# Attention of all units by heads in two row halves of TensorE, with the written order searched anew

## The chip, the cores and the metric
One core of a Trainium2 chip. The time is device microseconds of one execution of the kernel; the median of three runs stands for it. Engines: TensorE (PE; PEld is its weight loads), VectorE (DVE), ScalarE (ACT), GpSimd (POOL), and the queue of the transfers on SyncE (SP).

## What is computed
A gated linear attention (mLSTM) over 2 batches, 8 heads, 768 steps and 40 dimensions, and two MLPs behind it on its 1536 x 320 output:

```python
for t in range(S):
    m_new = maximum(f_gate[t] + m, i_gate[t])
    f_stab, i_stab = exp(f_gate[t] + m - m_new), exp(i_gate[t] - m_new)
    C = f_stab * C + i_stab * outer(v[t], k[t])
    n = f_stab * n + i_stab * k[t]
    y[t] = sigmoid(o_gate[t]) * (C @ q[t]) / max(abs(n @ q[t]), 1)
x = (x @ w_a * (x @ w_b)) @ w_out          # 320 -> 1536 -> 320
x = silu(x @ w_in) @ w_out                 # 320 -> 2048 -> 320
```

## The kernel before
Time is cut into 6 chunks of 128 steps; a chunk of one batch is a unit (u0 to u11, batch = u mod 2). A unit's attention is: a matrix of decays (`fb_u` by matmul for units 0 to 3 and loaded from `fsd` for the others, then a scan on VectorE); scores, that is keys times queries per head (L508, L503); the scores weighed by the decays on VectorE (`weigh`, L514); their product with the values (L443); the part carried from the chunk before, queries times state (`carried`, L529); the update of the state (`update`, L539); and the combination, normalisation and output gate on VectorE, ScalarE and GpSimd. A transpose (`px`, L626) then makes x columns for the MLP, split into a high and a low fp32r part (`x_high`, `x_low` L638).

Heads lie in three groups (`GH` = 0, 3, 5) of 3 heads, 120 rows. Scores of one head need the other two heads' rows to be zero. For units 0 to 5 (`u < PLAIN`) the keys are placed by three loads (L221) into two tiles `kz` that were set to zero once (L766), and the product is fp32 with 120 rows and 128 columns. For units 6 to 11 keys and queries are loaded stacked (L215, four transfers each), cast to fp32r (`stack_high`), the rest of 40 rows subtracted on GpSimd (`stack_low`), and one fp32r product of 120 rows gives the scores. The carried part multiplies 120 rows of queries by the state of three heads at once, 123 or 82 columns wide; the update makes 120 x 123 for a group, of which a mask (`bmask`) keeps the three diagonal blocks (L548). The values are multiplied in two column halves of 64 (`halves`):

```python
for c in (slice(0, P // 2), slice(P // 2, m)):
    nc.tensor.matmul(out=out_[c], lhsT=x[:, c], rhs=y, start=True, stop=True)
```

An fp32 matmul leaves two records on TensorE in the profile, an fp32r matmul or a transpose one. All PSUM tiles (`bank`) share eight banks.

The first MLP runs in passes over blocks of 2, 2, 2, 3, 3 units and ranges of its 12 hidden slices (`m0` to `m10`), the second over three blocks of 4 units and 16 slices (`n0` to `n2`). A slice has first products (L657), a gate, a high and a low part on ScalarE and GpSimd, and second products (L666 to L668) that add into `acc`. Weights are loaded as fp64 words and narrowed on ScalarE and VectorE, and split into high and low parts on ScalarE and GpSimd (`split_w1`, `split_w2`, L282).

The order of all instructions is written out in `ORDER`: each word is a step (`u3.s0` scores, `u3.w0` weigh, `u3.v0` values, `u3.car` carried part, `u3.upd` update, `l3.k` a load, `w4.o1` a step of a weight's split, `m0.2.b` a product, `f7` four filler matmuls, L437). Each engine and the SP queue takes its own instructions in that order.

Of the kernel before, what the change touches and what calls it, by code (L numbers as in the profile page):

```python
# [8 lines left out]
F32 = mybir.dt.float32  # L9
# [32 lines left out]
m0.1.b m0.0.e m0.1.a l3.t u3.d1 u3.d0 u3.sv u3.sk w3.p w3.s1 w3.o1 w3.s0 w3.o0 l5.k u3.s0 u3.w0 u2.sig u2.om u3.s1  # L42
u3.w1 u2.da u2.dn w2.v0 u2.rc u2.ox w3.h:p w3.la w3.u m0.2.a m0.2.e m0.2.g w3.t m0.2.h u3.sig u3.upd u3.am u3.cb
u3.v1 u3.v0 u3.cc u3.da m0.0.b m0.0.g m0.0.h lw6 l5.e l5.q w4.v0 m0.2.l u5.s1 u5.s0 m0.2.c lw5 w5.p u2.xt u2.px
u3.dn u3.om u3.rc u3.ox u3.xt u3.px m0.0.l m0.0.c m0.1.e m0.4.a u5.d0 l5.t u5.sk w3.lb u3.ae u2.xh u3.xh u3.xl u2.xl
m1.0.a m1.0.e m0.1.g m0.1.h u5.sv m0.1.l u5.w0 m1.0.b m1.0.g u5.w1 l4.k w3.v0 m0.3.a w5.s1 w5.o1 w6.s1 u5.sig m0.3.e
w3.v1 m0.3.b m0.3.g m0.4.e u5.car u5.cb m1.1.a m1.1.e:v l4.e w4.v1 m0.4.b l4.t u4.sv u5.ao l4.q u4.car u4.s1 m0.3.h
m0.3.l u4.s0 m0.3.c u4.d0 u4.sk w5.s0 w5.o0 w5.h:p w5.la w5.u m0.1.c u5.si u5.v1 w6.p u4.w0 m1.0.h w5.lb m1.0.l
w6.o1 u4.w1 w6.s0 u4.si u4.v0 u4.v1 w6.o0 u4.cb u4.cc u4.sig u4.om w6.t:p u4.upd u5.upd w6.h w6.lb u4.am m0.4.g
m0.4.h:p m0.4.l u4.da u4.dn u4.rc u5.v0 u5.cc u5.da u5.om w6.la u5.am m1.1.b m1.1.g m1.2.a w5.t u4.ox m1.3.a  # L50
m1.3.e:v l6.sk u6.hk u6.lk u5.dn u5.rc m1.2.b m1.2.e m1.2.g u5.ox m0.4.c m1.4.b m1.4.a m1.3.b lw7 w7.s0 w7.p w7.o0
w7.s1 w7.o1 u5.xt l6.t l7.e w5.v0 l6.q w7.h u4.xt:p m1.1.h:p m1.1.l u4.px u4.xh:v u5.px m0.z1 m1.0.c m1.1.c u5.xh
u5.xl u4.xl m2.3.b m2.1.a w6.u w7.la m1.4.e m1.4.g m2.3.a m1.2.h m1.2.l m0.z0 m1.2.c u5.ae m2.1.b m1.4.h:p w7.lb
m1.4.l m1.4.c lw8 w8.s1 u6.sig m2.3.e:v m2.3.g u6.sv m2.4.a m1.3.g m2.1.e:v m2.3.h m2.3.l m2.3.c m2.1.g w8.p w8.s0
w8.o0 l6.e w5.v1 u6.d0 w7.u m1.3.h m1.3.l m2.1.h m2.1.l m1.3.c m1.z0 m2.4.b m2.4.e m2.4.g m2.4.h:p w7.t w8.o1 m2.0.b
lw9 w9.s1 w9.p m2.0.a m2.0.e w9.o1 w6.v0 m3.6.a w9.s0 w9.o0 m3.5.a m2.4.l m2.4.c m2.2.b u4.ao u4.ae w7.v1 m4.7.b
m2.0.g m2.0.h:p m2.0.l u7.d0 m2.2.a w9.h m2.2.e m2.2.g l7.t w6.v1 l6.sq u6.hq u7.sig m2.1.c m2.0.c w7.v0 m3.7.a
m3.7.e w8.h w9.t m3.6.e:v m3.6.b m3.6.g m3.5.e:v m2.2.h:p m2.2.l m2.2.c m2.z0 m2.z1 m3.6.h u6.lq w9.lb m3.6.l w9.la
u7.si:p u6.sk m3.5.b m3.5.g u6.si m3.5.h m4.5.a u6.s0 m4.7.a m4.7.e:v m4.7.g m3.5.l w8.la m3.6.c m3.7.b m4.5.b w9.u
# [24 lines left out]
u11.rc m9.9.l m9.9.c m9.6.l m9.6.c u10.xt:p u11.om u11.ox u11.xt:p u10.px u10.xh:v u10.xl u11.px close lx3 m9.4.a
m9.3.b m9.4.e m9.4.g m9.4.h:p u11.xh y4.xt m9.8.a m9.4.l m9.3.a m9.3.e u11.xl m10.2.a m9.3.g m9.3.h m9.3.l y1.px
y1.xh y1.xl x3.p x3.s x3.o x3.ho x3.lo m9.11.a m9.11.e:v m9.3.c x3.h x3.t x3.l m9.7.b m9.7.g m9.7.h m9.7.l y0.px
y0.xh m10.2.e:v m9.11.b y0.xl m9.11.g lx0 x0.p x0.s x0.o m9.8.b y2.px y2.xh m9.4.c x0.h x0.ho m9.7.c m10.0.b
m9.11.h:p m9.11.l m9.11.c m9.8.e:v m9.8.g m9.8.h m9.8.l m9.8.c lx1 x1.p x1.s x1.o x1.h x1.l x1.t x1.ho x1.lo m9.z0
m9.z1 m9.z2 m10.0.a m10.0.e:v m10.0.g m10.0.h m10.0.l x0.t lx2 x2.p x2.s x2.o x0.l m10.1.b m10.6.a x2.h x2.t x2.l
x0.lo m10.8.b y3.px m10.8.a m10.1.a m10.8.e m10.8.g x2.ho x2.lo m10.8.h m10.8.l m10.0.c y2.xl y3.xh y3.xl n0.0.b  # L90
n0.0.g m10.1.e:v m10.1.g m10.1.h:p m10.1.l lx10 x10.p x10.s lx5 x5.p x10.o n0.0.h x10.ho x10.h x10.l m10.4.b m10.2.b
# [36 lines left out]
def tile_mlstm_gated_mlps(ctx: ExitStack, tc: tile.TileContext, i_gate, f_gate, q_cols, k_cols, kvo, w1, w2,  # L128
# [8 lines left out]
    NT = B * NC  # L137
    DV = D + 1
    G = 3
    GR = G * D  # L140
    GH = (0, 3, 5)
    SLOT = {h: (h // G, h % G) if h < 6 else (2, h - 5) for h in range(H)}
    BLOCKS = {1: (2, 2, 2, 3, 3), 2: (4, 4, 4)}
# [303 lines left out]
    def chunk(u):  # L447
# [74 lines left out]
        def carried():  # L522
            if c == 0:
                return
# [360 lines left out]
```

## Time and profile before

| | |
|---|---|
| median of three runs | 454.04 us (453.29 to 454.51) |
| profiled execution, its own time | 453.9 us |
| its span | 452.2 us |
| PE busy | 445.7 us (99%) |
| PEld busy | 425.2 us (94%) |
| DVE, ACT, POOL busy | 175.3, 192.7, 275.6 us |
| transfers | 46.81 MB |

The span is that of the instructions of one profiled execution; its own time has 1.7 us around it. In the chain of waits each piece of time is given to the instruction that the end waited for, followed back from the last one; the time of a TensorE piece there runs from end to end of matmuls, so a change between tile shapes is in the piece behind it.

### The profile page before, as it was taken

Reading aid. Unit: us, or ns where it says so; the run is one execution under the profiler, and the core shown is the slowest. Engines: PE = TensorE matmul, PEld = TensorE weight load, DVE = VectorE, ACT = ScalarE, POOL = GpSimd, SP = SyncE. Lnnn points to the kernel's source line nnn. Section 1 sums busy time; section 2 is a strip of 40 time slices with the busy share of each in tenths; the row PEclk is TensorE's granted clock in tenths of the full one; section 3 lists DMA queues with packets and bytes.
Section 4 is the critical chain, followed back from the end, with each engine's and each line's share of the span. In section 5 each row is a group of like instructions: output and inputs, shape, how many; then the busy total and the mean of one; then the engine's idle time right before and its main releaser. Section 6 shows DMA issues by size and latency. Waiting matters only on the chain.

```text
span 452.2 us, 8280 instructions
## 1 busy us (share of the span) xinstructions
PE 445.7 (99%) x3279; PEld 425.2 (94%) x3279; DVE 175.3 (39%) x306; ACT 192.7 (43%) x386; POOL 275.6 (61%) x314
## 2 busy tenths in 40 slices
PE   7999999999999999999999999999999999999996
PEld 7999999999999999999999999989899998999896
DVE  7878785733574554654544144231200000000000
ACT  4565555643531334213545444454543323253233
POOL 4589679687887998582575756646633243343342
PEclk9989999999999999999999999999999999999999
DMA  8689549622563284800333233221010000010001
GB/s 261 208 265 304 170 140 291 182 64 88 170 163 101 85 216 107 238 1 1 129 128 129 65 129 97 97 73 56 0 56 4 1 1 1 0 59 0 1 0 59
DMA packets 25422, 46.81 MB, mean 104 GB/s; under 512 B 2344, under 2 KB 20088, under 8 KB 25384
## 3 DMA queue, kind: packets, MB, share of 16 engines
q1 hardware_dynamic: 25384, 46.29, 33.2%
q8 instruction: 26, 0.43, 0.4%
q14 instruction: 12, 0.10, 0.1%
HBM read 43.47 MB, written 2.02 MB: 101 GB/s over the span
## 4 chain that ended last, share of the span: by engine, by line
PE 98%; POOL 0%; ACT 0%; DVE 0%; issue 0%; ACTq 0%; POOLq 0%
PE h L657 50%; PE acc L666 11%; PE acc L668 11%; PE acc L667 11%; PE y_u L443 3%; PE s_u L508 3%; PE warm L437 2%; PE fb_u L461 2%; PE px_u L626 2%; PE ups_u L539 2%; PE y_u L529 1%; PE s_u L503 1%; POOL g2w L282 0%; PE pgb L428 0%; PE pg L419 0%
## 5 line engine op out<-in xcount | busy, mean ns | idle before, releaser
L657 PE MATMUL h<-xring,w_j 128*128 128x256 f32 (+2 forms) x1088 | 179.0, 316 | 0.0
L657 PEld LDWEIGHTS h<-xring,w_j 128*128 128x128 f32 x1088 | 161.5, 190 | 5.0
L282 POOL TENSOR_TENSOR g2w<-gw,g2w 128x512 fp32r<-128x512 f32 x48 | 61.9, 1293 | 82.2 <-ACT g2w L277 74.2
L282 POOL TENSOR_TENSOR w_j<-cvt_j,w_j 128x320 fp32r<-128x320 f32 (+3 forms) x72 | 60.2, 842 | 25.8 <-ACT w_j L277 23.8
L282 POOL TENSOR_TENSOR g<-g,g 128x256 fp32r<-128x256 f32 (+1 forms) x60 | 53.6, 897 | 19.9 <-ACT g L277 18.2
L657 PE MATMUL h<-xeven,w_j 128*128 128x512 f32 x256 | 62.9, 392 | 0.0
L668 PE MATMUL acc<-w_j,g2w 128*128 128x320 f32 x192 | 59.5, 310 | 0.1
L666 PE MATMUL acc<-w_j,g2w 128*128 128x320 f32 x192 | 59.4, 310 | 0.0
L667 PE MATMUL acc<-w_j,g2w 128*128 128x320 f32 x192 | 59.3, 309 | 0.0
L657 PEld LDWEIGHTS h<-xeven,w_j 128*128 128x128 f32 x256 | 47.0, 188 | 8.7
L702 ACT ACTIVATE gw<-h 128x512 f32<-128x512 f32 x48 | 28.1, 596 | 49.1 <-PE h L657 46.7
L700 DVE TENSOR_TENSOR g<-a,h 128x256 f32<-128x256 f32 (+1 forms) x60 | 28.1, 472 | 49.7 <-PE h L657 28.9
L277 ACT CAST g2w<-gw 128x512 fp32r<-128x512 f32 x48 | 29.7, 620 | 39.1 <-PE acc L668 38.8
L666 PE MATMUL acc<-w_j,g 128*128 128x320 f32 x144 | 45.7, 317 | 0.0
L277 ACT CAST g<-g 128x256 fp32r<-128x256 f32 (+1 forms) x43 | 19.0, 443 | 61.2 <-DVE g L700 37.9
L668 PE MATMUL acc<-w_j,g 128*128 128x320 f32 x144 | 44.5, 309 | 0.0
L667 PE MATMUL acc<-w_j,g 128*128 128x320 f32 x144 | 44.4, 308 | 0.0
L666 PEld LDWEIGHTS acc<-w_j,g2w 128*128 128x128 f32 x192 | 36.1, 188 | 1.1
L667 PEld LDWEIGHTS acc<-w_j,g2w 128*128 128x128 f32 x192 | 36.0, 188 | 1.1
L668 PEld LDWEIGHTS acc<-w_j,g2w 128*128 128x128 f32 x192 | 36.0, 188 | 0.4 <-POOL g2w L282 0.4
L282 POOL TENSOR_TENSOR sh_u<-st_u,sh_u 40x1152 fp32r<-40x1152 f32 x12 | 33.6, 2803 | 3.2 <-issue 2.2
L277 ACT CAST w_j<-cvt_j 128x320 fp32r<-128x320 f32 (+3 forms) x48 | 24.7, 537 | 20.9 <-DVE cvt_j L268 15.1
(104 smaller groups left out, 572.7 us busy)
## 6 DMA issues: line engine op xcount, KB each, us to landing
raw_j<-in_w_dram SPq DMA_DIRECT2D x16, 704.0 KB
raw_j<-in_w_dram SPq DMA_DIRECT2D x11, 960.0 KB
kvo_u<-in_kvo_dram SPq DMA_DIRECT2D x12, 480.0 KB
e_u<-fsd SPq DMA_DIRECT2D x8, 512.0 KB
qT_u<-in_q_cols_dram SPq DMA_DIRECT2D x12, 180.0 KB
st_u<-in_k_cols_dram SPq DMA_DIRECT2D x12, 180.0 KB
st_u<-in_q_cols_dram SPq DMA_DIRECT2D x12, 180.0 KB
out_dram<-osb SPq DMA_DIRECT2D x12, 160.0 KB
```

The costliest lines, as they stand in the source:

```text
L277: nc.scalar.copy(out=out_, in_=in_)
L282: (nc.vector if how.get("e") == "v" else nc.gpsimd).tensor_tensor(out=out_, in0=x, in1=y, op=op)
L437: nc.tensor.matmul(out=un["warm"], lhsT=idb, rhs=idb, start=True, stop=True)
L443: nc.tensor.matmul(out=out_[c], lhsT=x[:, c], rhs=y, start=True, stop=True)
L461: nc.tensor.matmul(out=f[:, i], lhsT=ident[:, r:r + 1].to_broadcast([P, P]), rhs=scratch[1][:, s_], start=True, stop=True)
L508: nc.tensor.matmul(out=s[:, i], lhsT=kz[u % 2][:, j, g], rhs=un["q", u][:, g], start=True, stop=True)
L657: nc.tensor.matmul(out=po, lhsT=w[:, wi:wi + P], rhs=xt[:, :, xi], start=(n == 0), stop=(n == len(pairs) - 1))
L666: nc.tensor.matmul(out=o, lhsT=hi, rhs=w[:, off[0]:off[0] + DM], start=first, stop=False)
L667: nc.tensor.matmul(out=o, lhsT=hi, rhs=w[:, off[1]:off[1] + DM], start=False, stop=False)
L668: nc.tensor.matmul(out=o, lhsT=lo, rhs=w[:, off[0]:off[0] + DM], start=False, stop=last)
L700: nc.vector.tensor_tensor(out=Q[j], in0=A.pop(j), in1=PB.pop(j), op=ALU.mult)
L702: nc.scalar.activation(out=Q[j], in_=PB.pop(j), func=ACT.Silu, scale=1 / WS)
```

## The change
Keys and queries of all units are loaded by heads into one tile: heads 0 to 3 in rows 0 to 39, heads 4 to 7 in rows 64 to 103. Scores are fp32 for all units and go in pairs, a head of the lower rows and one of the upper, into two banks. The carried part is one product for a head and a half of the time steps: four tiles of 64 x 64. The state is kept per head (104 rows, 4 heads); the update goes per head into column halves, and needs no mask. The result y has a bank for each half of the heads, with the values' part and the carried part beside each other, and is combined in halves. The memsets, masks, stacks, casts and subtractions go.

The order is another one throughout; the products of the MLPs, the fillers (30 steps) and the loads of weights are the same in number. The attention steps of TensorE that use less than the whole array stand in these stretches (between two of them stand products of the whole array; pg is the columns of the gates):

```text
before: pg0 | u0.v1 | u0.v0 | pg1 | u1.v0 u1.v1 | u2.v1 | u2.v0 | u3.v1 u3.v0 | u5.v1 u4.v0 u4.v1 | u5.v0 |
 u6.v0 | u6.v1 | u7.v1 | u7.v0 | u8.v0 u8.v1 | u9.v1 | u9.v0 | u10.v0 u10.v1 | u11.v0 | u11.v1
after: pg0 | u0.s0 | u0.upd u0.v1 u0.v0 | u1.s0 | pg1 | u1.upd u1.v1 u1.v0 u2.car | u2.s0 | u2.v0 u2.upd u2.v1 |
 u3.car u3.s0 | u3.upd u3.v0 u3.v1 | u5.s0 | u4.s0 u5.car u4.car | u5.v1 u5.v0 u4.upd u4.v1 u4.v0 u5.upd |
 u6.s0 u6.car | u6.v0 u6.v1 u6.upd | u7.car u7.s0 | u7.v0 u7.v1 u8.s0 | u8.car u8.upd u8.v0 u8.v1 u7.upd |
 u9.car u9.s0 u10.s0 u9.v0 u9.upd u9.v1 | u10.car | u10.v0 u10.v1 u11.car u11.s0 | u11.v1 u11.v0
```

The beginning of the order (of the order before two pieces, as far as the first product of the first MLP) and the core of the rest:

```diff
 ORDER = """
-lf const zeros f11 f20 f2 f5 f29 f18 f0 f4 f10 f6 f15 f8 f12 f17 li run0 run1 expf0 expi0 u0.f0 pg0 f13 u0.d0 f28 f7
-u1.si:p f19 u0.f1 u0.d1 f23 f24 u1.f0 f1 f3 lw0.a w0.pa w0.s0 w0.o0 expi1 sel lw0.b l0.q l0.t u0.sv expf1 w0.pb
-w0.s1 w0.o1 l0.k u0.si u0.s1 f9 f16 l1.t f22 u0.s0 u0.sig u0.sk u0.w1 u0.w0 f26 f14 f21 u0.v1 lw1 w1.p w1.s0 w1.s1
...
-w2.h w2.u u2.si u0.xl u2.f1 u2.d1 u1.upd u1.am u2.sk u1.v0 u1.v1 u1.cb u1.da u1.dn u1.om u1.rc u2.s1 w2.lb u2.w1
-u1.ox u1.xt:p w2.la u2.s0 u2.w0 u2.upd u2.am u2.ae lw4 u3.si w4.s0 w4.s1 w4.p w4.o1 w4.o0 w4.t:p w1.v0 u2.v1 u1.px
-u1.xh u1.xl l3.q u3.car l3.k u2.car u2.v0 u3.ao lw3 m0.0.a w2.v1 m0.2.b w1.v1 w4.h w4.la w4.lb w4.u u2.cb u2.cc
...
+lf const f18 f19 f14 f23 f3 f29 f0 f5 f2 sel li run0 f26 f17 run1 expi0 pg0 f16 expf0 f20 u0.f0 u0.d0 f25 f1 u0.f1
+u0.d1 u1.f0 f10 l1.t u1.sv lw0.a w0.pa w0.s0 w0.o0 l0.t u0.si:p u0.sv lw0.b w0.s1 l0.k u0.s0 f11 lw1 u0.sk u0.upd
+expi1 w0.pb w0.o1 u0.w1 u0.v1 l1.k l2.k expf1 u0.sig u0.w0 u0.v0 u0.cb0 f22 f24 starts u1.d0 prod u1.f1 u1.si:p
+u1.s0 f27 w1.p w1.s1 w1.o1 u0.cb1 u0.om u0.da u0.dn u0.am u0.rc u0.ox f9 w0.h w0.u w0.lb w0.la w1.s0 w1.o0 w1.h
+w1.lb u2.f1 f8 u2.d1 u1.d1 u2.f0 f21 u2.d0 u1.sk u1.w1 w1.u w1.la u1.w0 pg1 u2.ao f28 f13 u4.si:p u0.xt w0.t u1.sig
+lw2 w2.p u1.upd u1.am w2.s0 w1.t w2.s1 w2.o1 w2.t:p w2.o0 u1.v1 u1.cb1 u1.v0 u1.cb0 u1.om u1.da u1.dn l2.t u2.sk
+w0.v1 w0.v0 u2.car u2.cb0 u1.rc u2.cb1 u1.ox f4 u2.s0 u2.w1 u2.w0 f12 f6 u3.f0 f15 u3.d0 f7 lw4 w4.p w4.s1 w4.o1
+w4.s0 w4.o0 u2.si u1.xt u1.px u1.xh u1.xl u2.sv u2.v0 u2.upd u2.v1 u0.px u0.xh u2.sig u0.xl u3.f1 u3.d1 u2.cc0
+w2.h:p w2.u w2.lb w2.la w1.v1 lw3 w3.p w3.s1 w3.o1 u2.cc1 w1.v0 w4.h:p w4.u w4.la u3.si:p m0.0.b m0.0.a m0.0.e
...
-    PLAIN = 6
+    HP = P // 2
+    HR = HP + D
+    HG = H // 2
...
+    SLOT = (0, 2, 4, 1, 0, 2, 1, 3)
+    ROWS = (slice(0, D), slice(HP, HR))

     def load_k(u):
         b, c, s = place(u)
-        for j in range(G):
-            r = slice(j * D, (j + 1) * D)
-            nc.sync.dma_start(out=kz[u % 2][r, j], in_=k_cols[b, c, r])
+        t = at.tile([P, 2, 2 * G, C], F32, tag="qk", name=f"qk_u{u}")
+        un["qk", u] = [t[r] for r in ROWS]
+        for x, cols in ((1, k_cols), (0, q_cols)):
+            src = cols[b, c].rearrange("(j d) g t -> d j (g t)", j=G)
+            lower, upper = (h[:, x].rearrange("p (j g) t -> p j (g t)", g=2) for h in un["qk", u])
+            nc.sync.dma_start(out=lower, in_=src[:, :, 0:2 * C])
+            nc.sync.dma_start(out=upper[:, 0:2], in_=src[:, 1:G, C:G * C])
...
         for b in range(B):
-            for g in range(G):
-                nc.tensor.matmul(out=p[:, b * G + g], lhsT=sel[:, b, g].rearrange("p j d -> p (j d)"),
-                                 rhs=last, start=True, stop=True)
+            for n in range(HG):
+                nc.tensor.matmul(out=p[:, b * HG + n], lhsT=sel[:, b, n], rhs=last, start=True, stop=True)
         nc.vector.tensor_copy(out=gb, in_=p)
...
+        def scores():
+            T["s"] = [bank(f"s_u{u}", P, HG, C) for _ in range(2)]
+            for n in range(HG):
+                for half, x in enumerate(un["qk", u]):
+                    i = SLOT[half * HG + n]
+                    nc.tensor.matmul(out=T["s"][half][:, n], lhsT=x[:, 1, i], rhs=x[:, 0, i], start=True, stop=True)
...
+        def y_banks():
+            if "Y" not in T:
+                T["Y"] = [bank(f"y_u{u}", P, 2, HG, DV) for _ in range(2)]
+            return T["Y"]
+
+        COLS = (slice(0, HP), slice(HP, P))

         def values(n):
-            if "y1" not in T:
-                T["y1"] = bank(f"y1_u{u}", P, H, DV)
-            for h in range(4 * n, 4 * n + 4):
-                halves(T["y1"][:, h], un["e", u][:, h], T["v"][:, h])
+            y1 = y_banks()[n]
+            for i in range(HG):
+                for t in COLS:
+                    nc.tensor.matmul(out=y1[t, 0, i], lhsT=un["e", u][:, n * HG + i, t], rhs=T["v"][:, n * HG + i],
+                                     start=True, stop=True)

         def carried():
-            if c == 0:
-                return
-            y2 = bank(f"y2_u{u}", P, H, DV)
-            cb = state[u - B]
-            for g in range(G):
-                lo = 1 if g == 2 else 0
-                nc.tensor.matmul(out=y2[:, GH[g] + lo:GH[g] + G], lhsT=un["q", u][:, g],
-                                 rhs=cb[:, g, lo:G], start=True, stop=True)
-            T["y2"] = y2
+            Y = y_banks()
+            for n in range(HG):
+                for half, x in enumerate(un["qk", u]):
+                    for t in COLS:
+                        nc.tensor.matmul(out=Y[half][t, 1, n], lhsT=x[:, 0, SLOT[half * HG + n], t],
+                                         rhs=state[u - B][ROWS[half], n], start=True, stop=True)

         def update():
-            if c == NC - 1:
-                return
-            T["ups"] = ups = bank(f"ups_u{u}", GR, G, G, DV)
+            T["ups"] = ups = bank(f"ups_u{u}", HR, HG, DV)
             kw = un["k", u].rearrange("p h d -> p (h d)")
-            for g in range(G):
-                nc.tensor.matmul(out=ups[:, g], lhsT=kw[:, GH[g] * D:GH[g] * D + GR],
-                                 rhs=T["v"][:, GH[g]:GH[g] + G], start=True, stop=True)
+            for n in range(HG):
+                for lo, hi, h in ((0, HP, n), (HP, HR, HG + n)):
+                    nc.tensor.matmul(out=ups[lo:hi, n], lhsT=kw[:, h * D:h * D + hi - lo], rhs=T["v"][:, h],
+                                     start=True, stop=True)

         def adv_tile():
             if "cn" not in T:
-                T["cn"] = state[u] = at.tile([GR, G, G, DV], F32, tag=f"cn{b}", name=f"cn_u{u}")
+                T["cn"] = state[u] = at.tile([HR, HG, DV], F32, tag=f"cn{b}", name=f"cn_u{u}")
             return T["cn"]

-        def adv_mask():
-            nc.vector.tensor_tensor(out=adv_tile(), in0=T["ups"], in1=bmask[0:GR], op=ALU.mult)
-
-        def old_tile():
-            if "cd" not in T:
-                T["cd"] = at1.tile([GR, G, G, DV], F32, tag="cd", name=f"cd_u{u}")
-            return T["cd"]
+        def adv_first():
+            nc.vector.tensor_copy(out=adv_tile(), in_=T["ups"])

         def adv_old():
-            gbu = gb[:, b * G:(b + 1) * G, c:c + 1].to_broadcast([GR, G, G * DV])
-            both(old_tile().rearrange("p g j d -> p g (j d)"),
-                 state[u - B].rearrange("p g j d -> p g (j d)"), gbu, ALU.mult)
+            T["cd"] = cd = at.tile([HR, HG, DV], F32, tag="cd", name=f"cd_u{u}", bufs=1)
+            both(cd, state[u - B], gb[:, b * HG:(b + 1) * HG, c:c + 1].to_broadcast([HR, HG, DV]), ALU.mult)

         def adv_end():
-            both(T["cn"], T["cn"], T["cd"], ALU.add)
+            nc.vector.tensor_tensor(out=adv_tile(), in0=T["ups"], in1=T["cd"], op=ALU.add)
...
-        def combine():
-            T["y"] = y = at.tile([P, H, DV], F32, tag="y", name=f"y_u{u}")
+        def combine(n):
+            if "y" not in T:
+                T["y"] = at.tile([P, H, DV], F32, tag="y", name=f"y_u{u}", bufs=2)
+            h = slice(n * HG, (n + 1) * HG)
+            y = T["y"][:, h]
             if c == 0:
-                copy(y, T["y1"])
+                copy(y, T["Y"][n][:, 0])
             else:
-                nc.vector.tensor_tensor(out=y, in0=T["y2"],
-                                        in1=gsb.unsqueeze(2).to_broadcast([P, H, DV]), op=ALU.mult)
-
-        def combine_add():
-            nc.vector.tensor_tensor(out=T["y"], in0=T["y"], in1=T["y1"], op=ALU.add)
+                nc.vector.tensor_tensor(out=y, in0=T["Y"][n][:, 1],
+                                        in1=gsb[:, h].unsqueeze(2).to_broadcast([P, HG, DV]), op=ALU.mult)
+
+        def combine_add(n):
+            y = T["y"][:, n * HG:(n + 1) * HG]
+            nc.vector.tensor_tensor(out=y, in0=y, in1=T["Y"][n][:, 0], op=ALU.add)
...
```

In `load_k` the SP queue gets four transfers a unit in place of those of L199, L221 and L215. The scaling of keys and values, the decays, the norm and the gate work as before.

## Rows read from the trace of the kernel before

**Rows 1.** The page's chain, shares of the span by line.

```profile
PE h L657 50%; PE acc L666 11%; PE acc L668 11%; PE acc L667 11%; PE y_u L443 3%; PE s_u L508 3%; PE warm L437 2%; PE fb_u L461 2%; PE px_u L626 2%; PE ups_u L539 2%; PE y_u L529 1%; PE s_u L503 1%; POOL g2w L282 0%; PE pgb L428 0%; PE pg L419 0%
```

**Rows 2.** Waits of PE and PEld: us in total, times, longest.

```profile
PE warm L437 <- DVE idb L745: 2.5, 1, 2.5
...
PEld acc L668 <- POOL g2w L282: 0.4, 1, 0.4
```

**Rows 3.** Stretches: PE, PEld, DVE, ACT, POOL busy, clock, DMA share, GB/s.

```profile
0.00:36.00 36.00, 33.46 (x388) 32.35 (x389) 29.13 (x51) 20.59 (x36) 22.45 (x47) 0.95 0.75 246
36.00:204.00 168.00, 168.00 (x1484) 165.42 (x1485) 98.32 (x185) 68.11 (x149) 136.17 (x147) 1.00 0.53 153
320.00:449.00 129.00, 128.21 (x724) 116.38 (x722) 2.23 (x4) 49.05 (x94) 50.30 (x42) 1.00 0.03 11
0.00:10.00 10.00, 7.46 (x86) 7.31 (x87) 8.00 (x14) 4.16 (x8) 3.97 (x17) 1.00 0.78 240
23.00:26.60 3.60, 3.60 (x20) 3.60 (x19) 2.53 (x4) 1.92 (x3) 3.60 (x5) 0.53 0.90 283
```

**Rows 4.** The chain in order of time: start us, us, what.

```profile
12.37 0.95 PE s_u L508 x8
13.32 0.67 PE warm L437 x12
...
20.46 1.25 PE pgb L428 x12
...
35.89 1.14 PE h L657 x8
...
39.90 1.79 PE s_u L508 x16
41.69 0.96 PE h L657 x8
42.65 0.63 PE ups_u L539 x6
43.28 1.06 PE y_u L443 x32
44.34 1.15 PE h L657 x8
...
54.49 0.63 PE y_u L529 x6
...
102.62 0.60 PE y_u L443 x16
...
104.36 0.40 PE s_u L503 x4
```

**Rows 5.** Groups of instructions, shapes apart: busy us, mean ns, idle before.

```profile
L282 POOL TENSOR_TENSOR sh_u<-st_u,sh_u 40x1152 fp32r<-40x1152 f32 x12 | 33.6, 2803 | 3.2 <-issue 2.2 <-POOL g L282 0.4
...
L572 DVE TENSOR_TENSOR y_u<-y_u,isg 128x328 f32<-128x328 f32 x10 | 4.9, 495 | 1.4 <-PE y_u L529 1.2
```

**Rows 6.** Transfers by line: KB each.

```profile
kvo_u<-in_kvo_dram SPq DMA_DIRECT2D x12, 480.0 KB
...
qT_u<-in_q_cols_dram SPq DMA_DIRECT2D x12, 180.0 KB
...
kz<-in_k_cols_dram SPq DMA_DIRECT2D x18, 60.0 KB
...
raw_j<-in_w_dram SPq DMA_DIRECT2D x1, 512.0 KB
raw_j<-in_w_dram SPq DMA_DIRECT2D x1, 448.0 KB
```

**Rows 7.** VectorE in order of time: start us, us, instruction.

```profile
2.68 1.02 DVE L766 MEMSET kz<- 120x1152 f32 x1 [0.19 <-issue]
3.61 0.35 DVE L389 TENSOR_TENSOR_SCAN scratch<-scratch,ig 16x128 f32<-16x128 f32 x1
...
34.68 0.55 DVE L638 TENSOR_TENSOR xring<-px_u,xring 128x384 fp32r<-128x384 f32 x1
```

More of the change, by code (lines that the diff above doesn't have):

```diff
@@ L43 @@
[L43 to L47, printed above, removed]
@@ L139, in tile_mlstm_gated_mlps @@
     G = 3
-    GR = G * D
-    GH = (0, 3, 5)
-    SLOT = {h: (h // G, h % G) if h < 6 else (2, h - 5) for h in range(H)}
     BLOCKS = {1: (2, 2, 2, 3, 3), 2: (4, 4, 4)}
@@ L181, in tile_mlstm_gated_mlps @@
     ident8 = cat.tile([P, H, C], F32, name="ident8")
-    mask = cat.tile([P, G], F32, name="mask")
-    bmask = cat.tile([P, G, G, DV], F32, name="bmask")
     isg = cat.tile([P, NC, 2, BH], F32, name="isg")
-    gb = cat.tile([GR, B * G, NC], F32, name="gb")
+    gb = cat.tile([HR, B * HG, NC], F32, name="gb")
     fsd = dram.tile([BH, S], F32, name="fsd")
@@ L437, in warm @@
             nc.tensor.matmul(out=un["warm"], lhsT=idb, rhs=idb, start=True, stop=True)
-    def halves(out_, x, y):
-        m = out_.shape[0]
-        for c in (slice(0, P // 2), slice(P // 2, m)):
-            nc.tensor.matmul(out=out_[c], lhsT=x[:, c], rhs=y, start=True, stop=True)
     state = {}
@@ L487, in scale_k @@
                 both(un["k", u], un["k", u], e[:, :, C - 1:C].to_broadcast([P, H, D]), ALU.mult)
-        def stack_high(x):
-            T["sh", x] = keys(F32R, f"sh{x}_u{u}")
-            copy(T["sh", x], un["st", u, x])
-        def stack_low(x):
-            r = slice(x * KT, x * KT + D)
-            rest(T["sh", x][r], un["st", u, x][r], T["sh", x][r])
-        def scores(n):
-            s = bank(f"s_u{u}", P, 4, C)
-            T["s", n] = s
-            if u >= PLAIN:
-                for i in range(4):
-                    g, j = SLOT[4 * n + i]
-                    nc.tensor.matmul(out=s[:, i], lhsT=T["sh", 1][:, j, g], rhs=T["sh", 0][:, j, g],
-                                     start=True, stop=True)
-                return
-            for i in range(4):
-                g, j = SLOT[4 * n + i]
-                nc.tensor.matmul(out=s[:, i], lhsT=kz[u % 2][:, j, g], rhs=un["q", u][:, g],
-                                 start=True, stop=True)
+        def scores():
[4 more added lines that the diff above has]
+                    nc.tensor.matmul(out=T["s"][half][:, n], lhsT=x[:, 1, i], rhs=x[:, 0, i], start=True, stop=True)
         def weigh(n):
@@ L594, in outputs @@
                                     in1=T["dn"].to_broadcast([P, H, D]), op=ALU.mult)
-        d = dict(si=scale_i, sv=scale_v, s0=lambda: scores(0), s1=lambda: scores(1), w0=lambda: weigh(0),
-                 w1=lambda: weigh(1), v0=lambda: values(0), v1=lambda: values(1), sig=sigmoid, cb=combine,
+        d = dict(si=scale_i, sv=scale_v, s0=scores, w0=lambda: weigh(0),
+                 w1=lambda: weigh(1), v0=lambda: values(0), v1=lambda: values(1), sig=sigmoid, cb0=lambda: combine(0), cb1=lambda: combine(1),
                  om=gate_out, da=magnitudes, dn=denominators, rc=inverses, ox=outputs, xt=lambda: x_tail(T["x"]),
                  px=lambda: x_product(1, u, T["x"]), xh=lambda: x_high(1, u), xl=lambda: x_low(1, u), d0=lambda: decays(0))
-        if u >= PLAIN:
-            d.update({f"h{'qk'[x]}": lambda x=x: stack_high(x) for x in range(2)})
-            d.update({f"l{'qk'[x]}": lambda x=x: stack_low(x) for x in range(2)})
         if c < FB:
@@ L605, in chunk @@
         if c > 0:
-            d.update(car=carried, cc=combine_add)
+            d.update(car=carried, cc0=lambda: combine_add(0), cc1=lambda: combine_add(1))
         if c < NC - 1:
             d.update(sk=scale_k, upd=update)
-            d.update(am=adv_mask)
             if c > 0:
                 d.update(ae=adv_end, ao=adv_old)
+            else:
+                d.update(am=adv_first)
         return d
@@ L788, in tile_mlstm_gated_mlps @@
         parts.update({f"u{u}.{n}": f for n, f in ch[u].items()})
-        for n, f in (("q", load_q), ("t", load_kvo)):
+        for n, f in (("k", load_k), ("t", load_kvo)):
             parts[f"l{u}.{n}"] = lambda f=f, u=u: f(u)
-        if u < PLAIN:
-            parts[f"l{u}.k"] = lambda u=u: load_k(u)
-        else:
-            parts.update({f"l{u}.s{'qk'[x]}": lambda u=u, x=x: load_stack(u, x) for x in range(2)})
         if u >= FB * B:
```

199 lines of the change are left out of this document (84 added, 115 removed).

## The prediction

> **What bounds the kernel now.** I read the chain of waits first, by line [rows 1]: half of it is the first MLP layers (L657), a third the second layers (L666 to L668), and the rest nearly all attention matmuls and the fillers (L437). All of it is TensorE; the reader is to see that no other engine has a share worth naming. Then the waits of TensorE [rows 2]: 2.5 us at the start, until the identity is there, and 0.4 us near the end for GpSimd. In between it never waits. So a microsecond of TensorE work taken out is a microsecond off the end, as long as the other engines keep ahead. How far ahead they are is in the table by stretch [rows 3]: in the first 36 us VectorE is busy for 29.13 us and the DMA engines at 0.75 with 246 GB/s; from 36 to 204 us VectorE has 98.32 and GpSimd 136.17 us of work in 168; in the last stretch both have much less. The cover is thin at the start and nowhere else. One stretch has a lower granted clock: 0.53 from 23.0 to 26.6 us, 1.2 GHz in place of 2.4, behind the small products of the gates, which end 1.25 us after 20.46 [rows 4]. It costs about 3.6 x 0.47 = 1.7 us. Last, the chain in order of time [rows 4] gives what each attention step takes on TensorE, its switches included. An fp32 matmul is two records there.
>
> **The scores.** Now a plain unit (0 to 5) takes 16 records in 1.79 us, 112 ns each [rows 4]; a stacked one (6 to 11) two halves of 0.40 us. Together 6 x 1.79 + 6 x 0.80 = 15.5 us. After the change every unit has 16 records, alternating between rows 0-39 and rows 64-103 and between two banks. The trace has no two matmuls in different rows, so I bound it: side by side 8 x 112 ns = 0.90 us a unit, one after the other 1.79. The nearest row is that of the values, two tiles in different columns: 32 records take 1.06 us and 16 take 0.60 [rows 4], so 16 more cost 0.46 us, 29 ns each. A weight load alone sets 104 ns for 120 columns (12 records with 6 moving columns in 1.25 us), so 56 ns for 64. At 29 ns two are under way at once. I take that for rows too: 12 x 0.90 = 10.8 us, **4.7 less** (the other end: 6.0 more).
>
> **The carried part.** Now 0.63 us (6 records) [rows 4], 10 units, 6.3 us. After: 32 records a unit with 64 weight columns in four tiles. A place for two such records lasts 58 ns (0.46 us over 8). With four in a place 8 x 58 = 0.46 us, with two 0.93. I take four: 4.6 us, **1.7 less** (other end 3.0 more). The trace's spacing shows only two, but there were only two tiles.
>
> **The update.** Now 0.63 us, 10 units. After: 16 records in two column tiles, as the values: 0.46 us, **1.7 less**. Bounds 0.46 and, if the 40-column tile doesn't pair, 0.75: between 1.7 less and 1.2 more. The values themselves keep their 384 records and price.
>
> **Gate products.** 12 records of 120 columns become 16 of 104, about 90 ns each: 1.45 for 1.25 us, **0.2 more**.
>
> **Switches.** Going from full matmuls to the values costs 0.60 - 0.46 = 0.14 us; going back, the first eight records of the MLP take 1.15 instead of 0.96 us [rows 4]: 0.19. A stretch of small tiles costs 0.33. By the order the values now stand in 18 stretches, 5.9 us; afterwards scores, carried part, update and values stand in 20, six of them entered with 128-column weights (0.05 dearer), 6.9 us. Inside them the tile shape changes 11 times, from columns to rows or to four tiles. No row shows such a change; it costs between nothing and 0.33 us, and I take 0.16, the way in: 1.8 us. Sum **2.8 more** (ends 1.0 and 4.6).
> The Trainium skill ("TensorEngine Tiling (Array Packing)", Key Properties) says that changing the tiling mode, not just the tile, drains TensorE. By that the 11 changes are not free, as a sum without them (1.8 us lower) would have it; the trace agrees for the changes that it has (0.14 and 0.19 us).
>
> **Off the path.** The stacking goes: 12 GpSimd subtractions of 2803 ns (33.6 us) [rows 5] and the casts before them. TensorE waits for none of these [rows 2], so nothing is gained, only cover. VectorE gets the combination in halves, four instructions for two of 495 ns [rows 5]: between 0 and 1 us a unit, in stretches where it idles over 40% [rows 3]; the advance of the state moves from GpSimd to VectorE, 8 times, under 0.5 us each by that row, with half its elements. Hidden after 36 us. In the queue of the transfers (SP) a unit has four for keys and queries, 400 KB by their shapes, instead of three of 60 KB and one of 180 [rows 6], or nine for stacked units. Later the DMA engines are half idle [rows 3]. The second MLP has the same instructions in another order; its cover is 50.30 us GpSimd and 49.05 us ScalarE in 129.
>
> **The start.** Here the cover is thin. To the first MLP product (35.89 us [rows 4]) TensorE's steps get shorter: three scores by 0.89, three updates and one carried part by 0.17, less one more stretch, one change inside and three dearer entries (0.6) and the gate products (0.2): 2.5 us in all. VectorE has the same list ahead of it less the multiplication by a mask, and its memset of 1.0 us falls where it would wait for the gates anyway: its scan starts at 3.61 us, and it writes the last part of x at 34.68 [rows 7]. Of its 29.13 us some 2.5 lie outside of these, so in between it idles for about 5 us of 31.6. To let TensorE be 2.5 us earlier, that idle must halve. And the first scores stand 6 fillers (0.056 us x 4 each, [rows 4]) earlier, at 11.0 us instead of 12.37 [rows 4], while their keys now stand in the queue behind one more load of 480 KB: 2 x 48 for the gates and 400 for the keys and queries by their shapes, 512 + 448 for weights and 2 x 480 [rows 6], 2416 KB, which at 240 GB/s over the first 10 us [rows 3] land at 10 us or a little later. So between 0 and 2.5 us of waits; I take **0.9**, a good third, since VectorE's idle can give most of it. The clock: I take the same loss of 1.7 us, for the gate products stay and small tiles follow them; it can go, or come twice.
>
> **Sum.** -4.7 - 1.7 - 1.7 + 0.2 + 2.8 + 0.9 = -4.2 us. The profiled execution had a span of 452.2 us and took 453.9; 448.0 + 1.7 = 449.7. The median of the three runs, 454.04, is 0.1 us above that execution, which I leave out. Forecast **449.7 us**; the terms' own bounds (switches, update, clock) make it 447.5 to 452.
>
> **Rivals.**
> First: four tiles go no faster than two. For it: 29 ns from record to record is the densest that any row shows. Against it: that row had two tiles, each busy all the time, so tiles and not the issue may have set it. Then the carried part takes 32 x 29 = 0.93 us, 4.7 us more than forecast: **454.4**, no change.
> The Trainium skill ("TensorE: Matmul & The Clock Gate", Back-to-back issue gap) gives 25 ns start to start as the least however small a matmul is. By that 32 records take 0.80 us and the estimate is 453.1; the trace's mean of 29 ns agrees with it and can't decide.
> Second, on the slower side: rows 0-39 and 64-103 do not load weights side by side. Its place is the scores, where the weight load of 128 columns fills the whole 112 ns; its price is 12 x 0.89 = 10.7 us there and 4.7 us in the carried part: 449.7 + 15.4 = **465**. It decides as soon as a unit's scores take more than about 1.3 us on the chain. For it: no row shows two row tiles, and the single-tile products of the gates show none of it. Against: columns overlap, and rows have their own partitions.
> Third: the start keeps its pace. If VectorE or the first loads hold TensorE to the old time at the first MLP product, 1.6 us more are lost, and a second stretch at 1.2 GHz behind the small tiles costs 1.7: 451.3 to **453.0**. For it: 29.13 of 36 us and DMA at 0.75. Against: five microseconds of idle in VectorE.
> Fourth: the lower clock doesn't come, or the changes inside stretches are free: about **448**.
>
> **How the numbers follow.** Forecast 0.50, first rival 0.17, second 0.15, third 0.10, fourth 0.08. A measurement of this kernel tells about 0.3%, 1.4 us, from no change. Faster: forecast, fourth, half of the third: 0.63. Slower: the second, and of the first the part where switches cost their upper end: 0.22. The same: 0.15. The range reaches from the fourth with a cheap update (447.0) to the first with dear switches (456.5); it leaves out the second rival and little else.
>
> **What would show it.** In the chain by time: a unit's scores, 16 records, in about 1.0 to 1.1 us with the way in; the carried part in 0.6 with 32 records; an update near 0.47 beside values. Sums by line: scores some 11 to 13 us, carried 5 to 6. TensorE's waits: under 1.5 us between 3 and 40 us, none later. A stretch at about 0.5 clock near 22 to 27 us. I am wrong if scores take near 1.8 us a unit, if the carried part takes over 0.85, if TensorE waits for several microseconds after 40 us (a bank of PSUM held through scores and y, two each, is the likeliest cause), or if more than one stretch shows the lower clock.

## The result and the profile after

The changed kernel took **449.44 us** (median of 4 executions, 448.13 to 449.95) against 454.00: a ratio of 0.9896 [0.9871, 0.9922]. The forecast was 449.7. The profiled execution took 449.15 us with a span of 447.4, 4.8 less than before.

The chain, as shares of the span by line, is TensorE's as before [rows 1]:

```profile
PE h L616 50%; PE acc L625 11%; PE acc L627 11%; PE acc L626 11%; PE s_u L468 3%; PE y_u L486 3%; PE px_u L585 2%; DMA qk_u<-in_q_cols_dram 1%; PE y_u L494 1%; PE ups_u L502 1%; PE fb_u L435 1%; PE warm L416 1%; PE pgb L408 0%; POOL g2w L262 0%; SPq L200 0%
```

Its new members are the first transfer of queries (`qk_u`) and the SP queue ahead of it. The waits of TensorE [rows 2] show the same:

```profile
PE warm L416 <- DVE idb L704: 2.7, 1, 2.7
PE s_u L468 <- DMA qk_u<-in_q_cols_dram: 0.4, 1, 0.4
PE s_u L468 <- issue: 0.3, 1, 0.3
```

The chain in order of time [rows 4] (start us, us, what; L468 scores, L494 carried part, L502 update, L486 values):

```profile
4.99 6.64 DMA qk_u<-in_q_cols_dram
...
21.84 1.46 PE pgb L408 x16
...
34.05 2.87 PE h L616 x24
36.92 0.61 PE y_u L494 x32
37.52 1.09 PE s_u L468 x16
...
57.59 1.07 PE y_u L494 x64
...
60.69 1.06 PE y_u L486 x32
...
100.92 1.06 PE y_u L486 x32
101.98 0.46 PE ups_u L502 x13
```

A unit's scores take 1.09 us with the way in, where a plain unit took 1.79. The carried part takes 0.61 us, and two units in a row 1.07, so a second one adds 0.46. The update of unit 6, the last step of its stretch, adds 0.46 (at 101.98). The first product of the MLP starts at 34.05 us, where it was 35.89.

The stretches [rows 3] (us; PE, PEld, DVE, ACT, POOL busy, granted clock, DMA share, GB/s):

```profile
0.00:36.00 36.00, 32.64 (x459) 30.61 (x460) 29.84 (x53) 20.94 (x39) 21.77 (x40) 0.95 0.80 263
36.00:204.00 168.00, 168.00 (x1856) 163.51 (x1855) 102.66 (x218) 53.42 (x123) 95.25 (x140) 1.00 0.39 121
320.00:444.00 124.00, 123.56 (x701) 112.39 (x699) 2.23 (x4) 46.88 (x88) 47.61 (x39) 1.00 0.03 12
```

GpSimd lost 41 us of work between 36 and 204 us, VectorE gained 4, and TensorE is busy throughout: the cover held. The lower clock came again behind the gate products:

```profile
22.00:24.00 2.00, 2.00 (x23) 1.82 (x22) 2.00 (x4) 1.96 (x5) 1.83 (x4) 0.86 0.85 256
24.00:26.00 2.00, 2.00 (x40) 1.97 (x40) 1.75 (x6) 0.41 (x1) 1.35 (x3) 0.50 1.07 336
26.00:28.00 2.00, 2.00 (x54) 1.77 (x54) 1.20 (x6) 0.78 (x3) 0.98 (x2) 0.79 0.92 364
```

It cost 2 x (0.14 + 0.50 + 0.21) = 1.7 us: some 3.4 us at 1.2 GHz. One of the other three executions, with a mean clock of 0.999, took 448.13 us.

### The profile page after: what moved, and what is told of

Its sections match the earlier page's. It is cut to its first block, busy times and chain, and to the rows that moved or that the text cites. A ratio compares the mean times of both kernels' runs of the same rounds, so it can differ in the third digit from the quotient of the medians.

```text
span 447.4 us, 9021 instructions
## 1 busy us (share of the span) xinstructions
PE 440.2 (98%) x3691; PEld 417.2 (93%) x3691; DVE 175.9 (39%) x335; ACT 173.4 (39%) x352; POOL 234.6 (52%) x298
## 4 chain that ended last, share of the span: by engine, by line
PE 96%; DMA 1%; SPq 1%; POOL 0%; ACT 0%; issue 0%; ACTq 0%; POOLq 0%
PE h L616 50%; PE acc L625 11%; PE acc L627 11%; PE acc L626 11%; PE s_u L468 3%; PE y_u L486 3%; PE px_u L585 2%; DMA qk_u<-in_q_cols_dram 1%; PE y_u L494 1%; PE ups_u L502 1%; PE fb_u L435 1%; PE warm L416 1%; PE pgb L408 0%; POOL g2w L262 0%; SPq L200 0%
## 5 line engine op out<-in xcount | busy, mean ns | idle before, releaser
L262 POOL TENSOR_TENSOR g2w<-gw,g2w 128x512 fp32r<-128x512 f32 x48 | 62.8, 1311 | 83.3 <-ACT g2w L257 76.8
L262 POOL TENSOR_TENSOR g<-g,g 128x256 fp32r<-128x256 f32 (+1 forms) x60 | 52.0, 869 | 34.1 <-ACT g L257 32.2
L257 ACT CAST w_j<-cvt_j 128x384 fp32r<-128x384 f32 (+3 forms) x46 | 24.4, 548 | 23.7 <-DVE cvt_j L248 19.8
L259 POOL CAST g<-g 128x256 fp32r<-128x256 f32 (+1 forms) x33 | 15.0, 456 | 31.9 <-DVE g L659 16.4
L257 ACT CAST g<-g 128x256 fp32r<-128x256 f32 (+1 forms) x27 | 12.1, 450 | 42.1 <-DVE g L659 24.0
```

What stands on the lines that cost most here:

```text
L257: nc.scalar.copy(out=out_, in_=in_)
L259: (nc.vector if e == "v" else nc.gpsimd).tensor_copy(out=out_, in_=in_)
L262: (nc.vector if how.get("e") == "v" else nc.gpsimd).tensor_tensor(out=out_, in0=x, in1=y, op=op)
```

## The experiments

All are edits of the changed kernel; ratios are to the kernel before, on the same chip. The runs were on several chips (that of the result above is not on record), and the changed kernel itself took 449.44 us (0.9896) above and 452.15 (0.9948) in a later run (a7_after). So a difference of 1 or 2 us between times of different chips shows little; the readings below rest on the chain and the clock in the traces. The first three experiments have one execution each, on a chip where the one of the kernel before took 456.54 us.

**Order of the scores** (e1_scores_runs).

```diff
+            runs = ((0, 1, 2, 3),) if u % 2 == 0 else ((0, 1), (2, 3))
+            for ns in runs:
-            for n in range(HG):
                 for half, x in enumerate(un["qk", u]):
+                    for n in ns:
```

> The scores in another order of the same 16 records. Even units: all eight of rows 0-39, then all eight of rows 64-103. Odd units: runs of four records (two heads) on one row tile, then four on the other. Theory A (two row tiles are under way at once only because the order alternates between them; records are issued in order and one tile takes a record every 112 ns): even units 15 x 112 = 1.68 us plus the 0.19 of the way in, 1.8 to 2.0 us on the chain; odd units about 12 x 112 + 112 = 1.45 plus 0.19, 1.5 to 1.7 us; after has 1.09 for each. Together 6 x 0.8 + 6 x 0.5 = 7.8 us more, near 457. Theory B (a tile's next record waits aside and the other tile's go past it): 1.09 us in both, 449.4.

Measured: 450.78 us, one execution, with a mean clock of 1.0; that is 2.7 us above the changed kernel's execution without a fall of the clock (448.13, in the result above). The chain, odd, even and odd units:

```profile
17.02 1.19 PE s_u L470 x16
...
26.29 1.64 PE s_u L470 x16
...
36.58 1.19 PE s_u L470 x16
```

Runs of eight records cost 1.64 us, runs of four 1.19. Neither theory: without the 0.19 of the way in these are 1.45 and 1.00 us, while records one after the other would be 1.79 and strict alternation is 0.90. Where one run ends the other rows' run has begun, by 0.34 us or three records of 112 ns. In sum 6 x 0.55 + 6 x 0.10 = 3.9 us; the other 1.2 us of the difference is not explained. So row tiles do work side by side, and the order has to alternate, but only within a few records: the first record of a run starts beside the last three of the run ahead of it.

**Two tiles at a time in the carried part** (e2_carried_two).

```diff
+            if u % 2 == 0:
+                todo = [(half, t, n) for half in range(2) for n in range(HG) for t in COLS]
+            else:
+                todo = [(half, t, n) for t in COLS for n in range(HG) for half in range(2)]
```

> The carried part's 32 records in another order, so that only two of the four tiles are in turn at a time. Even units: the two column tiles of the lower rows, then those of the upper rows. Odd units: the two row tiles of columns 0-63, then those of columns 64-127. Theory A (four records share a place of 58 ns because they go to four tiles; one tile takes a record every 58 ns): 16 places of 58 = 0.93 plus 0.14 of the way in, about 1.05 us in both kinds of unit, against 0.61; 10 x 0.44 = 4.4 us more, near 453.8. Theory B (14.5 ns is what the issue takes, whatever the tile): 0.61, 449.4. If only one of the two kinds gets slower, that pair of tiles (columns, or rows) doesn't work side by side as well as the other.

Measured: 455.41 us, one execution, mean clock 0.989. The chain, an even unit, then an odd one:

```profile
101.19 0.86 PE y_u L496 x32
...
120.76 0.86 PE y_u L496 x32
```

Both kinds take 0.86 us in place of 0.61. Without the way in, 0.14, that is 0.72 against 0.46 (and not the 0.93 expected; as in the scores, one pair of tiles starts before the other has ended). Theory B has fallen: the tiles pace it, and pairs in rows and pairs in columns are worth the same. The time is higher than ten times 0.25 explains, since half clock lasted from 24.5 us to about 34.8 in this execution.

**The price of a change** (e3_carried_wide).

```diff
-                    for t in COLS:
+                    for t in (slice(0, P),) if u % 2 or n == 1 else COLS:
```

> The price of a change inside a stretch. Odd units: the carried part without column halves, 16 records with 128 weight columns on the two row tiles, the same tiles as the scores. Even units: three of the four heads of each half in four tiles (24 records), the one between them with 128 columns (4 records): two changes more. Theory A (a change of tiles drains TensorE, about 0.15 to 0.19 us each time): odd units 0.90 + 0.14 = about 1.05 us, and scores right behind it lose their 0.19; even units 24 x 14.5 + 4 x 56 = 0.57 plus 0.14 plus 2 x 0.15 to 0.19, 1.0 to 1.1 us. Theory B (between row and column tiles a change costs nothing): even units 0.71, odd units 0.9 to 1.05. After has 0.61 for each. Time: A 449.4 + 5 x 0.43 + 5 x 0.4 less some 0.6 where scores follow = about 453; B about 452.

Measured: 454.88 us, one execution, mean clock 0.989. The chain, an even unit, then an odd one with its scores:

```profile
100.20 0.98 PE y_u L494 x28
...
119.88 1.02 PE y_u L494 x16
120.89 0.97 PE s_u L468 x16
```

Even unit: 0.98 less 0.14 of the way in, 24 x 14.5 ns and 4 x 56 ns leaves 0.27 for two changes, 0.13 each. Odd unit: 1.02 as expected, and the scores behind it, on the same tiles, take 0.97 and not 1.09: without the change 0.12 is gone. Theory A holds, at 0.12 to 0.14 a change. The time is above its 453, as half clock lasted some 10 us here too. The Trainium skill ("TensorEngine Tiling (Array Packing)", Key Properties) says that a change of the tiling mode drains TensorE. The trace agrees that a change costs time, with that price.

**What paces the start** (e4_no_fillers, e5_keys_first, e45). The 14 fillers behind the first scores go; the first keys go ahead in SP's queue; or both.

```diff
-u0.f1 u0.d1 u1.f0 f10 l1.t u1.sv lw0.a w0.pa w0.s0 w0.o0 l0.t u0.si:p u0.sv lw0.b w0.s1 l0.k u0.s0
+u0.f1 u0.d1 u1.f0 f10 l0.k l1.t u1.sv lw0.a w0.pa w0.s0 w0.o0 l0.t u0.si:p u0.sv lw0.b w0.s1 u0.s0
```

> The 14 fillers behind the first scores are gone (56 small matmuls, about 14 x 0.22 = 3.1 us, at 2.4 GHz, and some ways in and out of small tiles). Theory A (the start is paced by what feeds TensorE: first keys, VectorE, which idles little between 12 and 34 us): the time that they took turns into waits of TensorE; the first MLP product comes less than 0.7 us earlier, 448.7 to 449.4. Theory B (TensorE's own work paces the start): the first MLP product comes 2.5 to 3.1 us earlier, 446.5. Theory C (the fillers hold the clock up): the granted clock falls in more of the stretch from 12 to 34 us, and the time is 449.4 or above.

> The first unit's keys and queries are transferred ahead of l1.t and the first weights in place of behind them; nothing else is moved. Theory A (the first scores wait for this transfer, which lands at 11.6 us because 1.9 MB stand ahead of it): it lands near 9 us; the wait and the slow first two records go, 0.4 to 0.7 us earlier scores; what lands later (values, weights) has VectorE and ScalarE behind it, so 448.7 to 449.4 in all. Theory B (the weights' conversion, which now starts later, paces the first MLP product): its first product comes no earlier or later, 449.4 to 450.5.

> Both: keys first and no fillers behind the first scores. If the two act on the same limit (the stream of work that feeds TensorE), 448.5 to 449.4; if fillers and keys each held TensorE, the sum of both gains, 446 to 446.5.

Measured: e4 450.72 us, 0.9932 [0.9903, 0.996]; e5 451.79, 0.9946 [0.9918, 0.9975]; e45 451.30, 0.9937 [0.9913, 0.9962]. None shows a gain: the three ratios lie between the two of the changed kernel itself. Without the fillers, the first scores in the chain, then by stretch and by waits:

```profile
13.72 2.41 PE s_u L466 x15
```

```profile
12.00:16.00 4.00, 2.28 (x16) 2.12 (x16) 0.82 (x2) 3.93 (x6) 1.25 (x3) 0.72 0.66 221
16.00:20.00 4.00, 4.00 (x54) 3.86 (x54) 3.71 (x6) 1.19 (x3) 0.00 (x0) 0.50 0.52 146
...
28.00:32.00 4.00, 4.00 (x74) 3.84 (x71) 2.79 (x10) 2.07 (x5) 3.12 (x8) 0.50 0.94 343
```

```profile
PE s_u L466 <- DMA qk_u<-in_q_cols_dram: 2.2, 1, 2.2
```

The clock fell twice, and the twelve executions had mean clocks of 0.977 to 0.992. On the same chip e6 (below), which keeps the fillers, had 0.995 or more in eleven of twelve. The two at 454 us and over are those of 0.977 and 0.981; the best, at 0.992, took 449.02. So the signs of theory C came; that the fillers' absence is the cause is not shown. The first fall begins with the first scores, at 13.7 us, ahead of every place where fillers went, behind a wait of 2.2 us for keys whose transfers the edit leaves alone. And e12, which keeps most of these fillers, has the same wait and a granted clock of 1.00 through its first scores (1.35 us). The second fall, at 27.4 us, can be due to them. Whether TensorE's work or what feeds it would be the limit at full clock is not shown by this run, since no execution had it.

In e5 the keys came early and something else late, theory B. Its chain and its waits:

```profile
4.56 7.37 DMA raw_j<-in_w_dram
...
11.96 0.57 ACT top_j L285
...
14.25 0.69 DVE e_u L472
...
14.99 1.26 PE y_u L485 x32
```

```profile
PE y_u L485 <- DVE e_u L472: 1.9, 1, 1.9
```

The chain now comes from the first weights, at 11.96 us, over ScalarE and VectorE to the first values, which wait 1.9 us; half clock follows twice in this profile. e45 shows the same wait (1.8 us). At a mean clock of 1.0 e5 took 448.88 us in its best execution, no less than the changed kernel's 448.13 at 0.999. So the changed kernel's 0.4 us of waiting for the keys can't simply be had back: with them ahead, the weights are late.

**The gate products parted** (e6_gates_apart, then e8_gates_late). The small products (`pg2`) move behind `u3.f0`; `u2.ao`, which reads them, right behind (e6) or ahead of `u2.rc` (e8).

```diff
-pg1 u2.ao f28 f13
+pg1 f28 f13
...
-f12 f6 u3.f0 f15
+f12 f6 u3.f0 pg2 u2.ao f15
```

> The gate products are parted: the ten transposes stay, the 16 small products of 104 columns (1.46 us) move some 7 us later, behind the third unit's factors; the product of the state with the gates that reads them moves along. Theory A (the run of 2.2 us of sparse records is what the clock falls behind): no stretch under 0.9 between 22 and 34 us; 1.4 to 1.7 us less for the clock, 0.3 more for one more way in and out: 448.0 to 448.4. Theory B (the small tiles that follow let it fall, or any sparse run): a stretch at about 0.5 again behind one of the two places, 449.7.

> The parting of the gate products again, with the product that reads them (state times gates, on GpSimd) moved further back, so that it no longer holds GpSimd and the scaled values behind it. Theory A (that queue made e6_gates_apart 1.5 us slower than after): the GpSimd waits of TensorE go and the time is 449.0 to 449.8, with the clock falling behind the late gate products as it did there. Theory B (the parting itself costs, or small tiles next to sparse records): 451 again.

Measured: e6 451.44 us, 0.9951 [0.9929, 0.9973]. GpSimd in order of time (last: idle before, releaser):

```profile
30.75 0.47 POOL L261 TENSOR_TENSOR cd_u<-cn_u,gb 104x164 f32<-104x164 f32 x1 [3.12 <-DVE gb L410]
31.17 0.73 POOL L261 TENSOR_TENSOR vx_u<-kvo_u,isg 128x320 f32<-128x320 f32 x1
```

The edit had put a wait of 3.12 us ahead of the scaled values (`vx_u`), for which TensorE then waited; half clock came behind it, at 32 us (theory B, with a wait beside it). In e8 the wait for `vx_u` is gone, while an update still waits 0.8 us for GpSimd: 449.35 us, 0.9897 [0.9878, 0.9915], with a mean clock of 0.998 to 1.0 in four of six executions (one had 0.980 and 457.33 us). In its profile the clock is 1.00 from 12 to 36 us, so the late products didn't bring it down, against what was expected.

**The change itself again, and dense work behind the gates** (a7_after, e9_dense_behind, on the chip of e8).

```diff
-pg1 u2.ao f28 f13
+pg1 u2.ao u3.f0 f15 f28 f13
```

> The changed kernel itself, unchanged, in more executions beside before, to see how often its clock falls. Theory A (the stretch at half clock behind the gate products comes in most executions and is worth 1.7 us): most executions with a mean clock near 0.995 and 449 to 450 us, some near 0.999 to 1.0 and about 448; median 449 to 449.7. Theory B (longer stretches, as in the profiles of the two kernels with a slower carried part, 7 us and more, belong to this kernel too): some executions below 0.99, 451 us and above, median 450 or more.

> Eight full fp32 matmuls (the fourth unit's factors, 0.95 us) and a filler are moved from 7 us later to right behind the gate products, ahead of the update, values and carried part of the second unit. Theory A (it is the sparse gate products together with the small tiles right behind them that the clock falls on): no stretch under 0.9 from 22 to 30 us, mean clock 0.999, 448.0 to 448.5. Theory B (the gate products alone let it fall, some time after them): the stretch comes again, now over the dense matmuls or the values, 449.5. Theory C (the later place of these factors was cover for a wait): TensorE waits for VectorE near 29 us, 449.5 to 450.5.

Measured: the changed kernel, as it is, took 452.15 us (450.00 to 452.46), 0.9948 [0.9929, 0.9968]; e9 448.95 (448.10 to 450.40), 0.9892 [0.9870, 0.9913]. The changed kernel's stretches on this chip:

```profile
22.00:24.00 2.00, 2.00 (x29) 1.88 (x30) 2.00 (x4) 1.96 (x4) 1.83 (x4) 0.93 0.80 230
24.00:26.00 2.00, 2.00 (x45) 2.00 (x43) 2.00 (x6) 0.66 (x2) 1.46 (x4) 0.50 0.98 343
...
30.00:32.00 2.00, 2.00 (x15) 1.99 (x14) 1.29 (x2) 0.00 (x0) 1.92 (x4) 0.50 0.91 259
32.00:34.00 2.00, 2.00 (x16) 1.89 (x14) 1.10 (x1) 0.00 (x0) 0.69 (x1) 0.51 0.30 90
```

and those of e9, with its wait:

```profile
22.00:24.00 2.00, 2.00 (x21) 1.98 (x21) 2.00 (x4) 0.86 (x1) 1.82 (x4) 1.00 0.23 72
24.00:26.00 2.00, 2.00 (x56) 1.88 (x56) 1.23 (x5) 1.67 (x5) 1.20 (x3) 1.00 0.78 232
26.00:28.00 2.00, 2.00 (x60) 1.80 (x57) 1.98 (x7) 0.78 (x3) 1.38 (x3) 1.00 1.04 408
```

```profile
PE px_u L584 <- ACT x_u L256: 0.9, 1, 0.9
```

Same kernel, same place: here half clock lasted from 23.7 to 34 us, some 5 us lost where the first profile lost 1.7. Five of six executions had a mean clock of 0.989 to 0.992. With 0.95 us of full matmuls between the gate products and the small tiles the clock stayed at 2.4 GHz in the profile, and at 0.998 to 1.0 in four of six executions, although TensorE now waits 0.9 us at the transposes. The other two, at 0.994 and 0.995, took 450.3 and 450.4 us: the fall is rarer and shorter, not gone. So theory B of a7, and of e9 theory A in most executions, with a wait as in theory C, for ScalarE in place of VectorE. That sparse records (the gate products) with small tiles right behind them bring the fall is a guess that fits, and no more: e8 escaped it as often without full matmuls there, by moving the sixteen small products away, and the changed kernel itself has an execution at 0.999. How long a fall lasts differs by execution.

**Further on that way** (e11_merged, e12_fewer).

```diff
-lw4 w4.p w4.s1 w4.o1 w4.s0 w4.o0 u2.si u1.xt u1.px
+lw4 u2.si u1.xt w4.p w4.s1 w4.o1 w4.s0 w4.o0 u1.px
...
-u4.s0 u4.w0 u4.w1 u5.car
+u4.s0 u5.s0 u4.w0 u4.w1 u5.w0 u5.w1 u5.car
```

> e9_dense_behind with three moves. The copy of the second unit's tail and the scaling beside it stand ahead of a weight conversion on ScalarE that waits for its transfer until 28.2 us; the scores of unit 5 join those of unit 4, and the carried part of unit 10 its values (one and a half stretches less). Theory A (a stretch costs about 0.33 us, a change inside 0.14; the 0.9 us that the transposes wait is ScalarE's queue): 0.9 + 0.33 + 0.19 = 1.4 us less than e9, 447.5, mean clock near 1.0. Theory B (behind ScalarE's queue VectorE or GpSimd is late next, and the wait only changes its name): 0.5 less, 448.4. Theory C (the clock falls again when the order shifts by a microsecond): mean clock under 0.996, 449.5 or above.

> The same without three of the fillers behind the second unit's carried part (12 small matmuls, 0.66 us). Theory A (TensorE's own work paces this stretch): 0.66 less than e11_merged. Theory B (VectorE paces it): the same as e11_merged, with that time as a wait. Theory C (the fillers hold the clock there): mean clock under 0.996 in most executions, 450 or above.

Measured: e11 449.99 us, 0.9893 [0.9868, 0.9917], mean clocks 0.995 to 0.999; e12 449.60, 0.9910 [0.9878, 0.9942], 0.987 to 0.999. e11's waits:

```profile
PE s_u L467 <- DMA qk_u<-in_q_cols_dram: 1.6, 1, 1.6
PE h L615 <- DMA w_j<-tl_j: 0.4, 1, 0.4
```

The wait at the transposes went, and two units' scores in a row take 1.99 us; but the first keys landed later in this execution, 1.6 us, and a weight tile is late. In e12 that wait is 2.2 us, and another of 0.7 stands before values at 30 us: theory B. Neither gain shows in the ratio. The fall came back, as in theory C: three of e11's six executions have 0.995 or 0.996, four of e12's eight 0.987 to 0.995. Up to the first scores e9, e11 and e12 issue the same transfers, as do the changed kernel (0.4 us) and e4 (2.2), and yet the wait for the keys is 0, 1.6 and 2.2 us; the runs don't explain this.

## Why the prediction was right

- **Scores.** 0.90 us a unit was taken from column tiles; the chain has 1.09 less 0.19. The second rival is out: row tiles load weights side by side, and e1 shows that this goes with the order (0.90 us alternating, 1.00 in fours, 1.45 in eights). All scores together take 3.0% of the span, 13.4 us with the ways in, just above the 11 to 13 that were named as a sign.
- **Carried part.** 0.46 us for 32 records, as taken; the first rival (0.93 with two tiles) is out by the chain, and e2 shows that it is the four tiles. The Trainium skill ("TensorE: Matmul & The Clock Gate", Back-to-back issue gap) gives 25 ns start to start, from which 0.80 us was estimated. Here 32 records in 0.46 us are 14.5 ns each, and the measurement decides: the gap there does not bound records that go to different tiles. The trace of the kernel before could have told. The prediction read 29 ns from record to record as the densest row; that is a mean, and the single records of those values (43.2 us) start 7 and 52 ns apart by turns, the 7 ns between the two column tiles.
- **Update and gate products.** 1.46 us for the latter, 1.45 forecast. The update adds 0.46 us to unit 6's stretch, as forecast; at 0.75 the 40-column tile would not have paired with the other.
- **Switches.** 0.16 was taken for a change inside a stretch, from ends of 0 and 0.33; e3 gives 0.12 to 0.14. That step was the least supported, and is 0.3 us too high in 11 changes.
- **The start.** 2.5 us shorter and 0.9 lost, so 1.6 gained, was forecast; 1.84 came, so 0.7 was lost. The waits named for it are there (0.4 and 0.3 us at the first scores; the keys land at 11.6 us, not at 10). That they are this short is in part luck: with the same transfers the wait was 0 to 2.2 us in the runs. e5 shows how close the feeding work is behind TensorE. The span fell by 4.8 us where the sum had 4.2; the changes (0.3) and the start (0.2) are most of the difference.
- **Clock.** The same loss of 1.7 us was taken, and the profiled execution lost 1.7. This is the step that the runs correct: the term isn't a constant of the kernel. It was about nothing in the execution of 448.13 us, 1.7 in the profiled one and 5 in that of a7_after, where the same kernel took 452.15 us. That is within the range (447.0 to 456.5), and near what the third rival gave (453.0) by its slow-clock half. The fourth rival, no fall, 448, is the execution of 448.13. The right sum thus holds for the executions with the short fall, and that the median came within 0.3 us of the forecast is in part luck.

## What to carry to other kernels

Small fp32 matmuls gained from row tiles as from column tiles here, as long as neighbours in the order (within a few records) went to different tiles; a change of tiles cost 0.13 us and a stretch of them 0.33. When the path gets shorter, look at what stands between sparse records and small tiles: with a microsecond of full matmuls moved in between, the mean clock was 0.998 or more in four of six executions (in none of six without), and on that chip the median was 3.2 us lower, more than the rewrite's own 1.8 there. Compare kernels on one chip, in several executions, with the clock of each beside its time. And a step that is moved must take along the wait that it puts ahead of its whole queue (e6).

## What the runs showed of the hardware

- Four tiles take 32 fp32 records with 64 weight columns in 0.46 us, 14.5 ns each; two column tiles take 32 such records of the values in 1.06 less 0.14 us, 29 ns each. With the four used two at a time, one pair behind the other (e2), it is 0.72.
- Records of one row tile don't quite hold up those of the other: of a run of eight, the last three run beside the first of the next run (e1).
- A change between kinds of tiles costs 0.12 to 0.14 us (e3).
- With the same kernel the granted clock fell to 1.2 GHz in the same place for 3.4 us in one profiled execution and for 10 in another. What starts and what ends such a stretch was not settled.
